# Softmax sums in other banks, and a new order of the steps, in a recurrent memory-attention kernel

## The chip, the cores and the metric

The kernel runs on one core of a Trainium2 chip. The metric is the device time of one execution in microseconds (us). The engines are named as in the profile: PE (TensorE), DVE (VectorE), ACT (ScalarE), POOL (GpSimd) and SP (SyncE, which here issues most DMAs).

## The reference

Two kinds of layer alternate, A B A B, each with a residual sum and a layer norm in front. B (a gated MLP with a product over the sequence) is hardly touched. In A the 2048 rows are cut into 64 segments of 32 rows, and each segment attends over itself and over 8 memory rows, which are the first 8 output rows of the segment before:

```python
for s in range(n_seg):                       # 64 segments, one after the other
    xs = x[:, s * seg_len:(s + 1) * seg_len, :]
    h = jnp.concatenate([mem, xs], axis=1)   # 8 + 32 rows of 512
    q, k, v = (jnp.einsum('btd,dhe->bhte', h, W) for W in (Wq, Wk, Wv))   # 32 heads of 128
    scores = jnp.einsum('bhqe,bhke->bhqk', q, k) * scale
    scores = jnp.where(mask[None, None], scores, -1e9)
    p = _softmax(scores, axis=-1)
    o = jnp.einsum('bhqk,bhke->bhqe', p, v)
    o = jnp.einsum('bhte,hed->btd', o, Wo)
    mem = o[:, :M, :]                        # 8 rows, for the next segment
    outs.append(o[:, M:, :])
```

Weights and activations are bfloat16. So there are 128 segments in a row (64 in each of the two A layers), and each needs the result of the one before.

## The kernel before, in words

`a_block` is one A layer; `segment` (line 830) is one segment. Four segments (j4 = 0 to 3) make a block tb of 128 rows. The program's order on PE, DVE and ACT is the order in which it is written (`manual_schedule`, line 664); POOL's and SP's instructions are placed by the planner.

A segment begins when hA is ready: 32 rows, 8 of memory and 24 of its own, laid out as the stationary side of the projections. (The last 8 rows of each segment are projected ahead, for a whole block, as "old" rows: `b_units`, line 713. Their queries stand in QQ[:, :, :, 32:40], their keys in KX, their values in VX.) Then follow:

- **Projections.** `mm_chunk` (line 674) is 16 matmuls of 512 columns, four 32-column groups of PE by four parts of the contraction. `qk(0)` and `qk(2)` (first half r = 0 of the heads: queries and keys) and `qk(1)` go to three PSUM tiles of a bank each; `k_halves` (line 852) does the keys of the second half in two pieces of 256 columns in banks 0 and 1 of the tile psK; `v_mm(0)` puts the first value chunk into bank 2 of psK. ACT copies queries and keys to SBUF (lines 846, 862), DVE transposes them (lines 850, 864) into QQ and KA.
- **Scores** of both halves (`scores`, line 882, 20 matmuls each, tile psS), then the exponentials on ACT (line 894) into E and the mask on DVE (line 897). E has, per half, 160 columns of (4 heads x 40 rows) and 64 columns for the old rows (`own`). DVE copies the first value chunk (line 968). PE does the second value chunk `v_mm(1)` (psV), which ACT copies (line 980).
- **Softmax sums** by matmuls with ones: `sums_1` (line 899) for half 1 into psM, `sums_0` (line 909) for half 0 into columns 320 to 479 of each bank of psO. Then **PV** (`pv`, line 918) into columns 0 to 319 of psO.
- **Inverses** on ACT, as exp(-ln(sum)): Rm for the 8 memory rows, Rt for the 32 others (`log_of`, line 940, and `inverse`, line 944). DVE multiplies PV by Rm into uT_cur (`scaled`, line 947, source line 948) and later by Rt into uT_nxt (`tok_out`) and oB (`last_out`): the token rows of a segment are projected with the memory rows of the next.
- **Output projection** `wo_pass` (line 743): 128 matmuls into pw, half 1 of the heads first. DVE merges 8 memory rows of pw into the rows of the next segment and transposes them (`build_hA`, lines 821 and 822). ACT copies pw out (`store_o`, line 827), SP stores it.

PSUM's eight banks are used by tags: accA and accB have one bank each, att two, attO four; a tile waits until the readers of its tag's former tile are done. The framework orders accesses of different engines to one PSUM tile.

Between these steps the program puts work that isn't on the recurrence. `fill(n)` does n pieces of the block's projection of old rows (`b_units`, six chunks of 16 matmuls in three segments, in pieces of 4, 4, 8 and 16 matmuls) or of the output projection of old rows (`y_part`). `spare1` (line 1060) is on DVE: a row sum `y_add` (line 223), and at j4 = 3 a normalisation `apply` (line 197). `spare2` is on DVE too: statistics. `copies`, `turns` and `adds` are lists of small jobs of the filling chunks for ACT and DVE. `tail` (line 1092) issues DMAs.

The values of the old rows get into VX through HBM: `spread_v` (line 696) stores VB with one DMA and loads it in 16 DMAs of 16 KB. At the second A layer the old rows of block 0 are projected ahead, at the end of the B layer before (`_Ahead.chunks`, line 609); `wo.open` (line 574) then takes SBUF for Wo and loads it.

## Time and profile before

| | before |
|---|---|
| three runs | 2088.17, 2091.4, 2104.64 us (median 2091.4) |
| the profiled execution | 2106.03 us, span 2104.3 us |
| granted clock of PE, mean | 0.974 |
| busy: PE, PE weight loads, DVE, ACT, POOL | 80%, 50%, 56%, 52%, 8% |
| first and last start of the transpose that writes hA | 30.7 and 1950.5 us (128 of them) |
| DMA queue of SP | 107.17 MB in 205768 packets, 20.2% of 16 engines |

How to read it: the span is the profiled execution from its first to its last instruction. A busy share is a mean over all stages; matmuls are pipelined, so a busy PE need not be a full one. Lines of the timeline have the start in us, the duration, engine, source line, operation, the tiles written and read, the shape, the count, and in brackets the idle time of the engine just before, with what ended it. Lines of a group have busy time and mean duration in ns, and the idle time before them with its releaser. Where a helper makes an instruction, the line is the helper's.

### The profile page before, as it was taken

What the parts mean: (1) busy time and instruction counts of PE and PEld (TensorE: products, weight loads), DVE (VectorE), ACT (ScalarE), POOL (GpSimd) and SP (SyncE); (2) the same over time, 40 slices, a digit from 0 to 9 for tenths busy, and PEclk for the clock granted to TensorE, in tenths of its full rate; (3) what the DMA queues carried; (4) which work ended last, traced back from release to release, by engine and by line L of the source; (5) the groups of instructions that cost most, each with busy time, mean ns of one, the idle gap of its engine ahead of it and who ended that gap; (6) DMA issues with size and microseconds to landing.
All of it is one profiled execution on the core that took longest, in us unless ns stands there. A gap on an engine that the chain in (4) does not pass through costs nothing.

```text
span 2104.3 us, 106502 instructions
## 1 busy us (share of the span) xinstructions
PE 1686.2 (80%) x48827; PEld 1041.7 (50%) x48850; DVE 1170.6 (56%) x2754; ACT 1083.8 (52%) x2530; POOL 164.4 (8%) x388
## 2 busy tenths in 40 slices
PE   3777778887888787889987878887778777887999
PEld 1444445544554444446644544554444444544465
DVE  2455555565555565566455555555565555556742
ACT  1555655554555465554035555555455554555610
POOL 5000000000000000011200000000000000000200
PEclk9899999999999899999999999999999999999999
DMA  9101000011101111137951111011211012021777
GB/s 338 34 19 25 28 25 27 26 45 58 37 27 37 55 52 37 40 112 157 205 154 29 29 29 29 29 29 29 63 59 30 26 48 76 27 49 56 180 157 168
DMA packets 214825, 141.11 MB, mean 67 GB/s; under 512 B 138432, under 2 KB 186928, under 8 KB 214376
## 3 DMA queue, kind: packets, MB, share of 16 engines
q1 hardware_dynamic: 205768, 107.17, 20.2%
q0 software_dynamic: 8592, 27.12, 3.9%
q8 instruction: 382, 6.26, 1.3%
q14 instruction: 67, 0.55, 0.1%
q10 hardware_dynamic: 16, 0.01, 0.0%
HBM read 65.45 MB, written 41.92 MB: 51 GB/s over the span
## 4 chain that ended last, share of the span: by engine, by line
PE 58%; ACT 22%; DVE 13%; DMA 3%; issue 3%; SPq 0%; POOL 0%; DVEq 0%; POOLq 0%
PE pw L746 13%; PE psm L678 9%; PE pg L381 7%; PE psK L678 6%; ACT Rt L942 6%; ACT rows L862 5%; DVE KA L850 4%; PE psK L859 4%; PE pz L280 4%; PE psb L678 3%; ACT Rm L945 3%; ACT Rm L942 3%; ACT rows L846 3%; DVE E L897 2%; DVE uT L948 2%
## 5 line engine op out<-in xcount | busy, mean ns | idle before, releaser
L678 PEld LDWEIGHTS <-hA 128*32 128x32 bf16 x10240 | 266.2, 96 | 337.3 <-issue 104.6
L746 PEld LDWEIGHTS <-uT 128*32 128x32 bf16 x16384 | 259.4, 104 | 272.9 <-DVE uT L948 268.7
L746 PE MATMUL pw<-Wo_high,uT 128*32 128x128 bf16 x8704 | 183.7, 232 | 209.7 <-DVE uT L948 208.6
L846 ACT CAST rows<-psm 128x512 bf16<-128x512 f32 x384 | 225.1, 586 | 166.9 <-PE psm L678 166.8
L678 PE MATMUL psm<-Wq_sb,hA 128*32 128x512 bf16 x4096 | 277.2, 382 | 12.2 <-DVE hA L822 7.6
L948 DVE TENSOR_TENSOR uT<-psO,Rm 128x128 bf16<-128x128 f32 x256 | 62.4, 286 | 336.2 <-ACT Rt L942 336.2
L859 PE MATMUL psK<-Wk_sb,hA 128*32 128x256 bf16 x4096 | 161.4, 273 | 67.3 <-ACT rows L862 67.3
L850 DVE STREAM_TRANSPOSE QQ<-rows 128x512 bf16<-128x512 bf16 x256 | 180.8, 706 | 41.6 <-ACT rows L846 35.2
L678 PE MATMUL psK<-Wv_sb,hA 128*32 128x512 bf16 x2048 | 134.0, 380 | 60.2 <-ACT rows L862 60.2
L894 ACT ACTIVATE E<-psS 128x224 bf16<-128x224 f32 x256 | 77.6, 355 | 202.4 <-PE psS L890 202.4
L859 PEld LDWEIGHTS <-hA 128*32 128x32 bf16 x4096 | 112.4, 96 | 119.3 <-issue 93.3
L945 ACT ACTIVATE Rt<-Rt 128x512 f32<-128x512 f32 x256 | 158.8, 637 | 0.0
L381 PE MATMUL pg<-z,wspT 128*128 128x344 bf16 x1024 | 154.5, 309 | 0.4 <-DMA wspT<-in_B_w_sp_dram 0.4
L827 ACT COPY o_sb<-pw 128x128 f32<-128x128 f32 x126 | 33.5, 266 | 225.7 <-DVE pre L821 222.6
L746 PE MATMUL pw<-Wo,uT 128*32 128x128 bf16 x7680 | 147.3, 234 | 1.4 <-issue 0.7
L862 ACT CAST rows<-psK 128x256 bf16<-128x256 f32 x256 | 96.0, 375 | 92.3 <-PE psK L859 92.2
L948 DVE TENSOR_TENSOR uT<-psO,Rt 128x384 bf16<-128x384 f32 x256 | 139.8, 546 | 2.9
L678 PE MATMUL psm<-Wk_sb,hA 128*32 128x512 bf16 x2048 | 137.6, 381 | 2.5 <-DVE yB L775 2.5
L678 PE MATMUL psV<-Wv_sb,hA 128*32 128x512 bf16 x2048 | 136.1, 382 | 0.0
L968 DVE CAST VA<-psK 128x512 bf16<-128x512 f32 x128 | 88.5, 691 | 85.4 <-PE psK L678 85.4
L821 DVE CAST_PREDICATED pre<-maskM,pw 128x128 bf16<-128x128 uint16 x126 | 36.6, 291 | 174.5 <-PE pw L746 174.5
L864 DVE STREAM_TRANSPOSE KA<-rows 128x256 bf16<-128x256 bf16 x256 | 108.5, 424 | 41.5 <-ACT rows L862 41.3
(170 smaller groups left out, 2594.0 us busy)
## 6 DMA issues: line engine op xcount, KB each, us to landing
vb_d<-front SPq DMA_DIRECT2D x32, 256.0 KB
VX<-vb_d SPq DMA_DIRECT2D x512, 16.0 KB
o_d<-o_sb SPq DMA_DIRECT2D x126, 64.0 KB
ln_x<-xd SPq DMA_DIRECT2D x26, 256.0 KB
y_o<-o_d SPq DMA_DIRECT2D x22, 256.0 KB
xd<-y_o SPq DMA_DIRECT2D x22, 256.0 KB
y_x<-xd SPq DMA_DIRECT2D x22, 256.0 KB
Wq_sb<-in_A_Wq_dram POOLq DMA_DIRECT2D x8, 512.0 KB, 8.4
```

The source lines that it names most:

```text
L381: nc.tensor.matmul(pg[t][:, k, 0:344], lhsT=wsp[t][:, st, :], rhs=z(st, 344 * k, 344 * k + 344), start=(st == 0), stop=(st == NT - 1))
L678: nc.tensor.matmul(ps[32 * cg:32 * cg + 32, :], lhsT=lhs(kt, cg), rhs=rhs(kt, cg), start=(kt == 0), stop=(kt == KT - 1), tile_position=(0, ...
L746: nc.tensor.matmul(po[32 * cg:32 * cg + 32, 0:128], lhsT=lhs[:, _place(h), :], rhs=wo_rhs(h, cg), start=(h == WO_ORDER[0]), stop=(h == WO_ ...
L846: nc.scalar.copy(r[:], ps)
L850: nc.vector.transpose(out=QQ[:, j % 2, :, 0:32] if j < 2 else KA[:, j % 2], in_=r[:])
L859: nc.tensor.matmul(o[32 * cg:32 * cg + 32].rearrange("p (i c) -> p i c", i=2), lhsT=hA_cur[:, kt, :], rhs=qk_rhs(w, 3, kt, cg)[:, 2 * a:2 ...
L862: nc.scalar.copy(r[:, 256 * a:256 * a + 256], o)
L864: nc.vector.transpose(out=KA[:, 1, 8 * a:8 * a + 8], in_=r[:, 256 * a:256 * a + 256])
L942: nc.scalar.activation(out=t, in_=sview(r, lo, hi), func=ACT.Ln)
L945: nc.scalar.activation(out=t[:, r], in_=t[:, r], func=ACT.Exp, scale=-1.0)
L948: nc.vector.tensor_tensor(out=out, in0=o, in1=t[:, r].rearrange("p (g i q) -> p g i q", g=4, i=4)[:, :, :, lo:hi], op=ALU.mult)
L968: nc.vector.tensor_copy(VA[:, 0].rearrange("p i e -> p (i e)"), psK[:, 2, :])
```

## The change

- **Sums.** `sums_memory` (8 matmuls of 64 columns) sums only for the 8 memory rows, both halves, into columns 320 to 383 of psO's banks, ahead of PV. `sums_tokens` (8 matmuls) sums for the 32 other rows, both halves, into the two banks of a tile of its own, psT. ACT's logarithms become one for Rm (from psO, ahead of PV) and one for Rt (1024 columns, from psT).
- **Orders dropped.** `other_bank` tells the framework that a set of matmuls need not wait for a given read of the same tile, since it is in another bank: `qk(2)` against the copy of `qk(0)`, `v_mm(0)` against the copy of `qk(3)`, `scores(1)` against `exps(0)`.
- **Order of the segment.** The four query and key chunks run one after the other, and the keys of the second half are one chunk again. `scores(0)` and `exps(0)` come before `v_mm(0)`; then two pieces of filling, `scores(1)`, `exps(1)`, `v_mm(1)`, and `spare1`. The copy of the first value chunk goes from DVE to ACT, that of the second from ACT to DVE. Half 0 of the heads goes first in the scaling, the projection and the token rows; `last_out` is one operation for both halves.
- **Filling.** The chunks of `b_units` all use accA (the first block of the first layer apart); the value chunks come first and both in the first of the three segments.
- **Values of the old rows.** VX belongs to the Wo pools now. For block 0 of either layer it is filled on DVE by transposes (`regroup`), not through HBM. For later blocks the store comes a segment earlier and the 16 loads are issued 8 and 8 in the `tail` of segments j4 = 2 and 3.

```diff
-WO_ORDER = tuple(range(H // 2, H)) + tuple(range(H // 2))
...
+    def regroup(self, VB, VX):
+        for r in range(2):
+            t = self.rows.pool.tile([P, DM], BF16, name="ln_xn", bufs=2)
+            self.nc.vector.transpose(out=t[:], in_=VB[:, :, r, :])
+            t = t[:].rearrange("p (i b j k) -> p j b i k", i=4, b=4, j=4)
+            for j in range(4):
+                self.nc.vector.transpose(out=VX[:, j, r, :], in_=t[:, j])
...
-        for pair in ((0, 2), (1, 3), (4, 5)):
+        for pair in ((4, 5), (0, 2), (1, 3)):
...
+        def other_bank(mms, *reads):
+            for m in mms:
+                for r in reads:
+                    tc.declare_no_dep(m.ins, r.ins, reason="another bank of the tile")
...
-            for k, j in enumerate((0, 2, 1, 3, 4, 5) if early else (4, 0, 5, 2, 1, 3)):
-                if (early and k < 4) or k % 2 == 0:
-                    ps = (accA if k % 2 == 0 else accB).tile([P, 512], F32, name="psb")[:]
-                else:
-                    ps = att.tile([P, 512], F32, name="psb2")[:]
+            for k, j in enumerate((0, 2, 1, 3, 4, 5) if early else (4, 5, 0, 2, 1, 3)):
+                ps = (accB if early and k in (1, 3) else accA).tile([P, 512], F32, name="psb")[:]
...
+            def sums_memory(ps):
+                for k in range(2):
+                    for g in range(4):
+                        nc.tensor.matmul(ps[:, g, 320:384], lhsT=ones[32 * g:32 * g + 32, :],
+                                         rhs=e_own(32 * g, 32, 0) if k else e_all(32 * g, 32, 0, 8),
+                                         start=(k == 0), stop=True, tile_position=(32 * g, 0), skip_group_check=True)
+            def sums_tokens(ps):
+                for k in range(2):
+                    for sl in range(2):
+                        for g in range(2):
+                            o = ps[:, g, 256 * sl:256 * sl + 256].rearrange("p (n q) -> p n q", q=32)
+                            nc.tensor.matmul(o[:, :, 24:32] if k else o, lhsT=onesG[64 * g:64 * g + 64, sl, :],
+                                             rhs=e_own(64 * g, 64, 1) if k else e_all(64 * g, 64, 8, 40),
+                                             start=(k == 0 and sl == 0), stop=True, skip_group_check=True)
...
-            r0 = qk(0, accB.tile([P, 512], F32, name="psm")[:])
-            r2 = qk(2, accA.tile([P, 512], F32, name="psm")[:])
+            psQ = att.tile([P, 2, 512], F32, name="psQ")
+            r0, _, read = qk(0, psQ[:, 0, :])
+            r2, mms, _ = qk(2, psQ[:, 1, :])
+            other_bank(mms, read)
             qk_T(0, r0)
             qk_T(2, r2)
-            r1 = qk(1, att.tile([P, 512], F32, name="psm1")[:])
+            r1, _, _ = qk(1, accB.tile([P, 512], F32, name="psm")[:])
+            qk_T(1, r1)
             psK = attO.tile([P, 4, 512], F32, name="psK")
-            k1 = k_halves(psK)
-            ...
-            v_mm(0, psK[:, 2, :])
-            nc.vector.tensor_copy(VA[:, 0].rearrange("p i e -> p (i e)"), psK[:, 2, :])
+            r3, _, read = qk(3, psK[:, 0, :])
             psS = att.tile([P, 2, 512], F32, name="psS")
-            for r in range(2):
-                scores(r)
-            ...
+            scores(0)
+            expd = exps(0)
+            qk_T(3, r3)
+            close(0)
+            other_bank(v_mm(0, psK[:, 1, :]), read)
+            nc.scalar.copy(VA[:, 0].rearrange("p i e -> p (i e)"), psK[:, 1, :])
+            fill(2)
+            other_bank(scores(1), expd)
+            exps(1)
+            close(1)
             psW = accB.tile([P, 512], F32, name="psV")
             v_mm(1, psW)
-            fill(2 if first and s == 0 else 1)
-            nc.scalar.copy(VA[:, 1].rearrange("p i e -> p (i e)"), psW[:])
+            nc.vector.tensor_copy(VA[:, 1].rearrange("p i e -> p (i e)"), psW[:])
+            spare1()
...
             psO = attO.tile([P, 4, 512], F32, name="psO")
-            sums_0(psO)
+            sums_memory(psO)
+            Rm = segp.tile([P, 4, 64], F32, name="Rm", bufs=1)
+            nc.scalar.activation(out=Rm[:], in_=psO[:, :, 320:384], func=ACT.Ln)
+            nc.scalar.activation(out=Rm[:], in_=Rm[:], func=ACT.Exp, scale=-1.0)
+            psT = att.tile([P, 2, 512], F32, name="psT")
+            sums_tokens(psT)
             for r in range(2):
                 pv(r, psO)
-            ...
+            fill()
+            Rt = segp.tile([P, 4, 256], F32, name="Rt", bufs=1)
+            nc.scalar.activation(out=Rt[:].rearrange("p g n -> p (g n)"), in_=psT[:].rearrange("p g n -> p (g n)"), func=ACT.Ln)
...
             def tail():
+                if j4 in (2, 3) and tb + 1 < NB:
+                    for j in (0, 1):
+                        spread_v(blk_state[tb + 1], 2 * j4 - 4 + j)
```

## The prediction

> **What bounds the kernel now.** I read the page first: who is busy, and by whom the chain is made.

> ```profile
> span 2104.3 us, 106502 instructions
> PE 1686.2 (80%) x48827; PEld 1041.7 (50%) x48850; DVE 1170.6 (56%) x2754; ACT 1083.8 (52%) x2530; POOL 164.4 (8%) x388
> PE 58%; ACT 22%; DVE 13%; DMA 3%; issue 3%; SPq 0%; POOL 0%; DVEq 0%; POOLq 0%
> ```

> No engine is full, and the chain goes to and fro between PE, ACT and DVE: a recurrence of short dependent steps. The steps are the 128 segments. The ends of the transposes that write hA (line 822) lie 888.7 us apart from first to last in the first layer and 882.5 us in the second: 1771.2 us for 126 steps, 84% of the span. Cleanest steps take 13.0 us. Second view: the timeline of one segment; its first query matmul starts at 457.43.

> ```profile
> 460.03 0.61 PE L859 MATMUL psK<-Wk_sb,hA 128*32 128x256 bf16 x16
> 460.74 0.38 ACT L862 CAST rows<-psK 128x256 bf16<-128x256 f32 x1
> 461.17 0.62 PE L859 MATMUL psK<-Wk_sb,hA 128*32 128x256 bf16 x16 [0.53 <-ACT rows L862]
> ...
> 462.26 1.05 PE L678 MATMUL psK<-Wv_sb,hA 128*32 128x512 bf16 x16 [0.47 <-ACT rows L862]
> ...
> 463.71 0.61 ACT L894 ACTIVATE E<-psS 128x224 bf16<-128x224 f32 x2 [1.50 <-PE psS L890]
> ...
> 464.54 0.59 ACT L980 CAST VA<-psV 128x512 bf16<-128x512 f32 x1 [0.22 <-PE psV L678]
> ...
> 464.69 0.37 PE L906 MATMUL psM<-E,onesG 64*128 64x160 bf16 x8
> 464.99 0.28 PE L915 MATMUL psO<-E,ones 32*128 32x160 bf16 x8
> ...
> 466.26 0.58 ACT L942 ACTIVATE Rt<-psM 128x512 f32<-128x512 f32 x1
> 466.73 0.59 ACT L942 ACTIVATE Rt<-psO 128x512 f32<-128x512 f32 x1
> ...
> 467.36 0.49 DVE L948 TENSOR_TENSOR uT<-psO,Rm 128x128 bf16<-128x128 f32 x2 [2.13 <-ACT Rt L942]
> 467.70 1.08 PE L746 MATMUL pw<-Wo_high,uT 128*32 128x128 bf16 x64 [1.36 <-DVE uT L948]
> ```

> PE stands three times. The second half of the keys, and then the first value chunk, write psK only after ACT's copy out of another bank of psK: 0.53 and 0.47 us. After the sums PE has 0.36 us of PV and a piece of filling work and then stands until 467.70: DVE's scaling of the memory columns needs only PV and the inverse of the memory sums, ready at 466.35, but it reads psO, and ACT is still reading token sums of slice 0 out of psO until 467.32. From the first sum to the output projection it is 3.01 us. The groups say that this holds for all segments:

> ```profile
> L948 DVE TENSOR_TENSOR uT<-psO,Rm 128x128 bf16<-128x128 f32 x256 | 62.4, 286 | 336.2 <-ACT Rt L942 336.2
> L859 PE MATMUL psK<-Wk_sb,hA 128*32 128x256 bf16 x4096 | 161.4, 273 | 67.3 <-ACT rows L862 67.3
> ```

> **The rows I use.** A chunk of 16 matmuls holds PE for 0.865 us (starts 458.31 and 459.17). From PE's last start of a chunk's pace to ACT or DVE it is 0.23 us more; ACT to DVE 0.03; either to PE 0.05. A copy of 512 columns is 0.586 on ACT, 0.691 on DVE; a transpose of 512 0.706; an exponential of E 0.355; a mask 0.319; the scaling of 128 memory columns 0.286; Wo's 128 matmuls 1.80 (529.73 to 531.53 in the segment that starts at 519.47). On ACT and DVE an independent follower starts 0.09 us before the end. With these the old order, laid out instruction by instruction, gives a step of 13.07 us, beside the 13.0 seen; so I trust the same bookkeeping for the new one.

> **Front half of the segment, new.** Time 0 is the first query matmul. The four chunks run without a stop and end at 3.46: the halves of the keys are gone, and the order against ACT's read of the other bank is dropped. ACT copies the last at 3.69 to 4.28, DVE transposes it 4.31 to 5.01. Meanwhile PE does the scores of slice 0 (0.16: 20 matmuls, half of 463.12 to 463.45), the first value chunk to 4.49 and two pieces of filling (0.43) to 4.92, so the wait for the keys' transpose is covered but for 0.14. Where there is no filling (first segment of early blocks) that cover is gone, and PE waits 0.57 at the same place, with no later end. Scores 1 end at 5.22, exponential 5.45 to 5.81, mask 5.84 to 6.16, sums from 6.21; the second value chunk lies behind the scores and ends at 6.09. Before, the sums began at 464.69, so at 7.26: **1.05 us gained**. The copy of the first value chunk moves to ACT, between the two exponentials: 4.72 to 5.30, done before the second has its scores (5.45). The other copy goes to DVE, 6.32 to 7.01.

> **Back half, new.** Memory sums: 8 matmuls of 64 columns, 0.11 as the 8 of slice 0 now take (464.99 to 465.10). Added wait: PV, and behind it filling and projection, now waits for ACT's logarithm over the same banks. It starts at 6.55; 256 columns lie between 0.278 (128) and 0.579 (512), on the line 0.378: done at 6.92. The token sums fill that time: between 0.30 as now and 0.43 (1280 columns for 896); I take 0.43, to 6.75. PV 6.97 to 7.37, with the second half's values ready at 7.01 while its matmuls start at 7.17. Memory inverse done at 7.37 (0.419, between 0.310 and 0.637). Scaling 7.60, projection 7.94: 1.73 after the first sum instead of 3.01, **1.28 us gained**. The token logarithm (one of 1024 columns, 0.98 as the two of 512 take) is off that path, since it reads its own banks. Projection to hA is unchanged: it ends at 9.74, the filling chunk at 10.60, hA at 10.60. **A step is 10.65 us**, 2.42 less than 13.07. PE's own work in it is 9.98, so it is nearly the bound.

> [...] The 8 of slice 0 start 14 ns apart here. [...]

> **Added or moved work that may show.** (a) All filling now goes through accA, one bank: the last chunk waits for ACT's copy of the piece before, done at 9.43 against 9.74. A margin of 0.3, cost nothing; if ACT is later, PE is late by the excess. (b) DVE: row sums and normalisation (0.68 and 0.41) now stand between the value copy and the scaling, and two statistics (0.86 each) ahead of the merge into hA; laid out, blocks with both lose 0.7 per four steps, some 17 of 32 blocks: +12. (c) SP: the 16 VX loads of a block, 0.6 to 0.69 each, go 8 and 8 to the ends of two segments. Now they hold up a row load in four steps:

> ```profile
> 478.02 3.37 SPq L702 DMA_DIRECT2D VX<-vb_d  x5
> ...
> 482.59 0.64 SPq L219 DMA_DIRECT2D y_o<-o_d  x1
> 485.77 0.69 DVE L223 TENSOR_TENSOR y_o<-y_o,y_x 128x512 f32<-128x512 f32 x1 [7.77 <-DMA y_o<-o_d]
> ```

> These four steps are 32.4 us over. With 8 loads (5.2 us) instead of 16 ahead, the row arrives some 10 us into the segment, 3 to 4 late: 17 left, bounds 0 and 50. (d) Regrouping the first values on DVE: 2 x (0.706 + 4 x 0.311) = 3.9, once per layer. In the first layer it replaces 8.4 us of waiting for VX (49.3 to 57.8) and saves perhaps 6; at the second it falls among DVE work that PE doesn't wait for, bounds 0 and 3.9, taken as 2. POOL's queue is passed by nothing. (e) Instruction fetch. The chain shows such stops:

> ```profile
> 505.34 1.00 issue
> ```

> Above 13.07 per step the 126 steps hold 124 us: 32.1 in the two first ones, 32.4 for the rows, 59.7 else, mostly such stops. PE's idle time falls from 3.2 to 0.7 us a step, so stops hidden now will show. Bounds: -10 (a few instructions fewer) and +126 (a stop of 1.0 in each step); nearest to what is seen, 0.47 a step, I add +30.

> **The sum.** 126 x 10.65 = 1342; firsts 26; rows 17; stops 90; DVE 12; regrouping 2: 1489 for 1771, so -282. The profiled execution took 2106.0, so 1824; it lies 0.7% above the median of the three runs (2091.4). Scaled alike: **1812 us**. Its own range is 1765 to 1860.

> **Rivals.** *Fetch takes it*: PE, without pauses, stops 1.0 us in each step. For: pauses are where fetches hide. Against: most fetches pass without a stop even through the projection. +96 on the sum: 1907 us. *The dropped orders remain* in effect, that is, the change doesn't do what it says, and PE waits for each read of a neighbouring bank: the layout gives 12.08 a step, +180: 1990. Against: the waits above are exactly between such reads and writes of one tile. *Slower*, by one mechanism: denser matmuls bring the granted clock down. The place is PE's 9.98 us a step; at 0.75 they are 13.31, a step 13.98, about 2227. It decides from a step of 12.89, that is from a clock of 0.82. Against: a stretch with PE 81% busy (520 to 533) is granted 1.00, and the low clock, 0.63, is at 478 to 492, around the 7.8 us wait; idleness, not density, brings it.

> [...]

> **Numbers.** Forecast 0.64, fetch 0.17, orders 0.13, no change 0.02, slower 0.04. The first three are faster by over 1% (about what a measurement here can tell from no change): 0.94. The range, 1765 to 1895, takes the forecast's own and reaches half way into the fetch case.

> **What would show it.** Right: steps of 10.6 to 11.1 us; no wait of the memory scaling for a token logarithm; no wait of PE between the key chunks and the first value chunk; PE over 85% busy; sums to projection about 1.7 us. Wrong: a step over 11.5; PE waiting for ACT's copy ahead of the last filling chunk; DVE's row sum waiting for its load in more than four steps; "issue" above 6% of the chain; a lower clock.

## The result, and the profile after

The kernel after takes 1821.6 us (1819.2 to 1823.8), the kernel before 2095.3 us (2088.2 to 2104.6): a ratio of 0.869 with a 95% interval of 0.865 to 0.873, so 274 us less. The profiled execution after took 1823.8 us. From the page of the kernel after, the lines on the span, on who is busy, on the queue that brings instructions (packets, MB, share), and on the chain:

```profile
span 1822.1 us, 101610 instructions
PE 1652.9 (91%) x46779; PEld 959.6 (53%) x46802; DVE 1136.2 (62%) x2518; ACT 1037.1 (57%) x2018; POOL 164.0 (9%) x388
q8 instruction: 366, 6.00, 1.4%
PE 80%; issue 6%; DVE 5%; DMA 4%; ACT 4%; POOL 0%; SPq 0%; DVEq 0%; ACTq 0%; POOLq 0%
```

PE's busy time hardly falls; its idle time does. ACT goes from 22% of the chain to 4%, DVE from 13% to 5%: PE is the bound now. What doubles, from 3% to 6%, is "issue", time in which an engine waits for nothing that the profile shows. The timeline of one of the cleanest steps; its first query matmul starts at 551.75 (columns: start, duration, engine, line, operation, and in brackets the idle time before it and what ended that):

```profile
551.75 1.05 PE L689 MATMUL psQ<-Wq_sb,hA 128*32 128x512 bf16 x16
...
554.35 1.04 PE L689 MATMUL psK<-Wk_sb,hA 128*32 128x512 bf16 x16
...
555.34 1.03 PE L689 MATMUL psK<-Wv_sb,hA 128*32 128x512 bf16 x16
...
556.05 0.71 DVE L864 STREAM_TRANSPOSE KA<-rows 128x512 bf16<-128x512 bf16 x1 [0.15 <-ACT rows L861]
...
556.82 0.28 PE L887 MATMUL psS<-QQ,KA 128*32 128x40 bf16 x16
...
557.93 0.24 PE L912 MATMUL psO<-E,ones 32*128 32x64 bf16 x8
...
558.10 0.45 PE L922 MATMUL psT<-E,onesG 64*128 64x256 bf16 x8
558.22 0.38 ACT L985 ACTIVATE Rm<-psO 128x256 f32<-128x256 f32 x1 [0.66 <-PE psO L912]
...
558.64 0.42 ACT L986 ACTIVATE Rm<-Rm 128x256 f32<-128x256 f32 x1
558.66 0.28 PE L930 MATMUL psO<-E,VA 32*128 32x40 bf16 x16
...
558.96 1.00 ACT L993 ACTIVATE Rt<-psT 128x1024 f32<-128x1024 f32 x1
...
559.35 0.49 DVE L995 TENSOR_TENSOR uT<-psO,Rm 128x128 bf16<-128x128 f32 x2 [0.61 <-PE psO L934]
559.70 1.02 PE L761 MATMUL pw<-Wo,uT 128*32 128x128 bf16 x60
```

First sum 6.18 us after the first query matmul (7.26 before), projection 1.77 after the first sum (3.01 before). The first value chunk (555.34) has no wait ahead of it. DVE scales (559.35) while ACT is still in the logarithm of the token sums (558.96 to 559.96), which before had to end first. The groups say it for all segments (busy, mean ns of one, idle time before and what ended it):

```profile
L995 DVE TENSOR_TENSOR uT<-psO,Rm 128x128 bf16<-128x128 f32 x256 | 62.5, 285 | 65.4 <-PE psO L934 65.2
L689 PE MATMUL psK<-Wv_sb,hA 128*32 128x512 bf16 x2048 | 135.4, 380 | 0.0
L222 DVE TENSOR_TENSOR y_o<-y_o,y_x 128x512 f32<-128x512 f32 x24 | 16.4, 684 | 7.5 <-DMA y_o<-o_d 7.5
```

The scaling waited 336.2 us for ACT before; now it waits 65.2 us, and for PE. From the first to the last hA of each layer the 126 steps take 741.2 + 745.7 = 1486.9 us (before 1771.2): 284 us less, while the rest of the span is 2 us longer. So the gain is all in the steps. Their cleanest are 10.66 us, but their median is 11.58 in the first layer and 11.81 in the second.

### The profile page after: what moved, and what is told of

Its sections match the earlier page's. It is cut to its first block, busy times and chain, and to the rows that moved or that the text cites. A ratio compares the mean times of both kernels' runs of the same rounds, so it can differ in the third digit from the quotient of the medians.

```text
span 1822.1 us, 101610 instructions
## 1 busy us (share of the span) xinstructions
PE 1652.9 (91%) x46779; PEld 959.6 (53%) x46802; DVE 1136.2 (62%) x2518; ACT 1037.1 (57%) x2018; POOL 164.0 (9%) x388
## 4 chain that ended last, share of the span: by engine, by line
PE 80%; issue 6%; DVE 5%; DMA 4%; ACT 4%; POOL 0%; SPq 0%; DVEq 0%; ACTq 0%; POOLq 0%
PE pw L761 15%; PE psQ L689 12%; PE psK L689 11%; PE psb L689 8%; PE pg L380 8%; PE psm L689 6%; PE psV L689 4%; PE pz L279 4%; PE pwB L773 3%; ACT Rm L985 3%; PE psO L930 3%; PE psS L887 3%; PE py L423 2%; PE psO L912 1%; DMA wspT<-in_B_w_sp_dram 1%
## 5 line engine op out<-in xcount | busy, mean ns | idle before, releaser
L861 ACT CAST rows<-psQ 128x512 bf16<-128x512 f32 x256 | 149.8, 585 | 130.4 <-PE psQ L689 130.4
L864 DVE STREAM_TRANSPOSE KA<-rows 128x512 bf16<-128x512 bf16 x256 | 181.4, 709 | 37.1 <-ACT rows L861 32.3
L689 PE MATMUL psQ<-Wq_sb,hA 128*32 128x512 bf16 x2048 | 139.7, 382 | 13.4 <-DVE hA L837 7.8
L689 PE MATMUL psQ<-Wk_sb,hA 128*32 128x512 bf16 x2048 | 140.3, 381 | 2.1 <-issue 1.9
L689 PE MATMUL psm<-Wq_sb,hA 128*32 128x512 bf16 x2048 | 138.9, 380 | 0.5 <-issue 0.5
L689 PE MATMUL psK<-Wk_sb,hA 128*32 128x512 bf16 x2048 | 138.1, 379 | 0.0
L380 PEld LDWEIGHTS <-wspT 128*128 128x128 bf16 x1024 | 100.7, 98 | 59.0 <-DMA wspT<-in_B_w_sp_dram 5.0
L899 DVE TENSOR_TENSOR E<-E,maskN 128x224 bf16<-128x224 bf16 x256 | 72.2, 282 | 95.0 <-ACT E L896 95.0
L993 ACT ACTIVATE Rt<-psT 128x1024 f32<-128x1024 f32 x128 | 128.7, 1005 | 0.0
L689 PEld LDWEIGHTS <-hB 128*32 128x32 bf16 x2976 | 75.4, 97 | 83.5 <-DVE hB L613 25.2
```

The lines of the kernel that those rows point to most:

```text
L380: nc.tensor.matmul(pg[t][:, k, 0:344], lhsT=wsp[t][:, st, :], rhs=z(st, 344 * k, 344 * k + 344), start=(st == 0), stop=(st == NT - 1))
L689: return [nc.tensor.matmul(ps[32 * cg:32 * cg + 32, :], lhsT=lhs(kt, cg), rhs=rhs(kt, cg), start=(kt == 0), stop=(kt == KT - 1), tile_posi ...
L861: return r, mms, nc.scalar.copy(r[:], ps)
L864: nc.vector.transpose(out=QQ[:, j % 2, :, 0:32] if j < 2 else KA[:, j % 2], in_=r[:])
L899: nc.vector.tensor_tensor(out=E[:, r], in0=E[:, r], in1=maskN[:], op=ALU.mult)
L993: nc.scalar.activation(out=Rt[:].rearrange("p g n -> p (g n)"), in_=psT[:].rearrange("p g n -> p (g n)"), func=ACT.Ln)
```

## The experiments

All ratios are to the kernel before. "Step" is the mean of the 122 steps behind the first two of each layer. "Stops" needs a word. A pause is counted here from one start on PE to the next, so it is somewhat longer than the idle time in the brackets of a timeline. In the kernel after, of 80 pauses of PE over 0.45 us that nothing in the profile ends, 79 fall at one place of PE's instruction stream, within each layer the same modulo 256 (matmuls, weight loads and the sequencer's instructions counted); in the kernel before all 23 do. The column is the sum, over the 126 steps, of unexplained pauses over 0.3 us at that place.

That PE waits there for its instructions can be read from the packets of the queue q8. The kernel after has 46779 matmuls, 46802 weight loads and 109 sequencer instructions on PE, 93690 in all, which fill 366 times 256 places, and q8 has 366 packets of 16 KB. Matched in order, one packet to a place, nowhere in its steps does PE pass such a place sooner than 1.1 us after the end of its packet, and every long stop at one ends 1.1 to 1.7 us after it.

| kernel | us | ratio (95%) | step, us | us per 256 PE instructions | stops, us |
|---|---|---|---|---|---|
| before | 2095.3 | 1 | 13.82 | 4.82 | 26 |
| new back half only | 2015.4 | 0.960 (0.956-0.964) | 13.10 | 4.57 | 98 |
| new front half only | 2037.3 | 0.968 (0.963-0.973) | 13.20 | 4.81 | 11 |
| after, orders kept | 1981.1 | 0.944 (0.940-0.948) | 12.85 | 4.69 | 89 |
| after | 1821.6 | 0.869 (0.865-0.873) | 11.61 | 4.23 | 98 |
| after, wide projection | 1721.0 | 0.820 (0.817-0.822) | 10.87 | 5.46 | under 3 |
| back half, wide projection | 1909.7 | 0.909 (0.906-0.912) | 12.29 | 5.81 | under 3 |
| before, wide projection | 2067.9 | 0.984 (0.982-0.986) | 13.50 | 6.38 | 3 |
| first padding, "good" place | 1900.3 | 0.904 (0.901-0.907) | 12.32 | 4.11 | 157 |
| first padding, "bad" place | 1911.6 | 0.910 (0.907-0.913) | 12.31 | 4.10 | 170 |
| second padding, "good" place | 1850.8 | 0.881 (0.878-0.883) | 11.88 | 3.96 | 111 |
| second padding, "bad" place | 1900.7 | 0.905 (0.902-0.908) | 12.20 | 4.07 | 156 |
| front half, pause filled | 1923.9 | 0.917 (0.914-0.919) | 12.46 | 4.25 | 30 |
| after, VX loads together | 1821.8 | 0.868 (0.866-0.869) | 11.59 | 4.23 | 96 |

The theory at the start was the prediction's sum: both halves of the segment get shorter, and instruction fetch takes some of it back. The rivals: the dropped orders do all of it; the halves are worth little by themselves; the fetch stops are something else.

### Parts of the change

**New back half only**: the old kernel with the memory sums, the token sums and their inverses as in the new one, and half 0 of the heads first (the edit is shortened here).

```diff
-            sums_1(psM); sums_0(psO)          # and the four logarithms of slices 1 and 0
+            sums_memory(psO)                  # one logarithm of 256 columns, one inverse
+            sums_tokens(psT)                  # own banks; one logarithm of 1024 columns
...
```

> The old kernel with the new back half alone: memory sums ahead of PV in psO's spare columns, token sums in psT, one logarithm each, half 0 first in scaling and projection. The front half of the segment, its fillings and the VX loads are the old ones. My theory (two cuts on one path that add): first sum to projection falls from 3.0 to 1.75 us, the clean step from 13.0 to about 11.75 us, the time to about 1955 us (1935 to 1975). Rival (the back half is all of the gain, the front's new order only shifts waits): about 1830 us. Rival (the steps gain from the front, the sums were hidden anyway): about 2090 us.

2015.4 us. The cleanest steps are 11.79, as laid out, but the run is 60 us over what was expected. The waits of PE (total, times, longest):

```profile
PE psK L859 <- ACT rows L862: 67.2, 128, 0.8
PE psK L678 <- ACT rows L862: 60.1, 128, 0.5
PE pw L746 <- issue: 56.0, 57, 2.0
```

The first two lines are the front's waits, which this kernel keeps. The third is new: the projection stops in 57 places with no releaser, 56 us. Stops went from 26 to 98 us, as many as in the full change. The mechanism of the back half is right, and some 70 us of its gain are eaten by fetch.

**New front half only**: the new kernel with the old sums, inverses and order of heads (the edit is shortened).

```diff
-            sums_memory(psO)
-            sums_tokens(psT)
+            sums_1(psM)
+            sums_0(psO)
...
```

> The new kernel with the old back half: sums of half 1 in psM, of half 0 in psO, memory logarithm of half 0 behind PV, half 1 first. Front half, dropped orders, fillings and VX loads are the new ones. My theory: the clean step goes from 10.67 to about 11.95 us, since DVE again waits for ACT's token logarithm in psO; the time to about 1950 us (1930 to 1985). Rival (the back half is all of the gain): about 2090 us. Rival (the front is all): about 1825 us. Theory and both rivals together: the two halves' gains, measured against the old kernel, sum to the whole, 274 us, if they lie on one path one after the other.

2037.3 us, nearly 90 over the expectation. Part of it is a wait that the layout had not seen:

```profile
PE pw L762 <- DVE uT L951: 204.8, 128, 2.2
...
PE psO L925 <- DVE VA L984: 12.9, 81, 0.2
```

The first is the old pause ahead of the projection, kept. The second is PV, which comes earlier behind the sums here than DVE's copy of the second values: 0.16 us in 81 steps, so cleanest steps of 12.11 to 12.19 for 11.95. The rest is the clock. The granted clock is 0.935 on the mean; with stretches of 1 and of 0.5 alone, as the trace has them, that is 2 x 0.065 x 2019 = 262 us at half speed (before 0.974, 109 us; after 0.993, 26 us), and half of the steps have 13.66 to 13.88 us. Six stretches of this kernel (columns: stretch, its length, PE busy and matmuls, granted clock, DMA share, GB/s):

```profile
503.20:506.61 3.41, 1.68 (x92) 1.00 0.11 29
506.61:510.02 3.41, 3.41 (x120) 0.50 0.10 29
510.02:513.43 3.41, 3.41 (x68) 1.00 0.27 96
513.43:516.85 3.42, 3.40 (x104) 1.00 0.36 105
516.85:520.26 3.41, 1.67 (x88) 1.00 0.27 77
520.26:523.67 3.41, 3.41 (x128) 0.50 0.05 12
```

In this trace the clock changes in stretches of 3.41 us. Each of the two in which PE is busy for half of it (1.68 and 1.67 us) is followed by one at half speed (0.50), where the projection then is slow: in a step further on it takes 3.44 us (602.45 to 605.89), in the old kernel at full clock 1.98 (529.73 to 531.71). That makes the step 13.65 us long, which is four stretches, so the pause meets the same place of the next stretch again: the kernel is locked to it.

**Front half, pause filled**: this theory of the clock, tested with work that fills the pause and gives nothing (its bank is started anew by the projection).

```diff
+            for k in range(24):
+                g = k % 4
+                nc.tensor.matmul(pw[32 * g:32 * g + 32, :], lhsT=c["zeros"][:], rhs=wo.high[:, 0, :],
+                                 start=(k < 4), stop=(k > 19), tile_position=(0, 32 * g))
             wo_pass(pw, uT_cur)
```

> The new front half with the old back half, and 24 matmuls of 512 columns by zero weights in the pause ahead of the projection (their bank is started anew by the projection). Theory (the pause of 1.5 us comes at the same place of each 3.41 us window of the clock, since the step is four windows long, and the half clock that follows holds the step at that length): no window at half clock, steps 12.1 to 12.2 throughout, time 1955 to 1980 for 2037. Rival (the clock has nothing to do with the pause): 2037 or, with the added matmuls late, more.

1923.9 us: 113 us less, by adding 24 matmuls of 512 columns to every step, and below the expected range. The clock is 0.998, the median step 12.25. The same stretches:

```profile
503.20:506.61 3.41, 3.41 (x164) 1.00 0.02 5
506.61:510.02 3.41, 3.41 (x88) 1.00 0.09 24
510.02:513.43 3.41, 3.24 (x116) 1.00 0.02 5
```

So with the pause filled the front half is 171 us faster than the old kernel, without it 58, and what hid the difference was the clock. How much of the 171 the filling would give the old kernel, which has 109 us at half speed of its own, no run shows.

**After, with the orders between banks kept**: nothing of the schedule is changed, only the declarations dropped.

```diff
         def other_bank(mms, *reads):
-            for m in mms:
-                for r in reads:
-                    tc.declare_no_dep(m.ins, r.ins, reason="another bank of the tile")
+            pass
```

> The new kernel with all three dropped orders kept (the declaration is left out), all else new. My theory: the second query or key chunk waits for ACT's copy of the first, the first value chunk for the copy of the last key chunk, the second scores for the first exponential; laid out this gives a clean step of 12.08 instead of 10.67 us, and 1821 + 126 x 1.41, less some 30 us of fetch stops that hide in the new pauses: about 1970 us (1950 to 2000). Rival (the order of the steps does it, and the waits between banks were short enough to hide): below 1850 us.

1981.1 us, cleanest steps 12.08, both as the layout had it. PE waits for ACT's read of the neighbouring bank, at the second chunk and at the first value chunk:

```profile
PE psQ L689 <- ACT rows L859: 88.2, 128, 0.9
PE psK L689 <- ACT rows L859: 70.4, 127, 0.6
```

The third dropped order, at the second scores, shows no wait for ACT. With the orders kept 159.5 of the 273.7 us are lost; the rest of the change alone gives 114.2.

### The stops

**After, with a wide projection**: 32 matmuls of 512 columns in place of 128 of 128, the same columns in all. PE's step has about 511 instructions in place of 703 (the expectation says 539 and 731). This kernel and the next two leave out the sum over the four partial results.

```diff
-            for h in range(H):
-                for cg in range(4):
-                    nc.tensor.matmul(po[32 * cg:32 * cg + 32, 0:128], lhsT=lhs[:, _place(h), :], rhs=wo_rhs(h, cg), ...)
+            for i in range(H // 4):
+                for k in range(4):
+                    nc.tensor.matmul(po[32 * k:32 * k + 32, :], lhsT=lhs[:, _place(4 * i + k), :], rhs=..., ...)  # 512 columns
```

> The new kernel with the output projection as 32 matmuls of 512 columns instead of 128 of 128: each quadrant of pw gets the product of every fourth head over all columns, and the sum over the four quadrants is left out, so the projected rows are partial sums. PE's columns stay the same (32 x 54 ns = 1.73 us for 1.80), its instructions fall from about 731 to 539 a step. My theory: the stops of PE without a releaser (106 us in the 126 steps, 62 of them at the projection) are waits for instructions; most of those at the projection go: about 1750 us (1735 to 1770). Rival (the stops come from something that goes with the work, not with the count of instructions): 1821 - 9, about 1812 us.

1721.0 us, still below what was expected. From its page:

```profile
span 1721.0 us, 77034 instructions
q8 instruction: 270, 4.42, 1.1%
PE 83%; DVE 6%; DMA 5%; ACT 4%; issue 2%; POOL 0%; SPq 0%; DVEq 0%; ACTq 0%; POOLq 0%
```

No pause of PE over 0.45 us is left without a releaser. The cleanest steps hardly change (10.61 for 10.66), so it is not that the projection got shorter; the median does (10.7 for 11.6 to 11.8). 96 fetches fewer, and the stops are gone.

**The wide projection in the old kernel, and with the new back half** (the same edit).

> The old kernel with the projection in 32 matmuls of 512 columns (the sum over its four partial results is left out). Theory: the old kernel has only some 26 us of fetch stops, since its pause ahead of the projection hides them, so it gains little: 2045 to 2075, and the change is worth some 335 us where no fetch stops it, against 276 where it does. Rival (the wide projection gains some 100 us in any kernel): 1990 to 2005.

> The old front half with the new back half, and the projection in 32 matmuls of 512 columns in place of 128 of 128 (the sum over its four partial results is left out). Theory (the new back half alone gained 82 us and not more because its steps run into fetch stops): stops fall from 115 us to below 25, clean step 11.7, time 1895 to 1920. Rival (the wide projection gives what it gives by shortening the projection, 0.04 us a step): 2005 to 2015.

2067.9 and 1909.7 us, both as expected. In kernels without stops the change is worth 2067.9 - 1721.0 = 347 us: 158 for the back half and 189 for the front on top of it. (The clock has a part in these: the three kernels have 99, 66 and 30 us at half speed.) With stops it is worth 274. The 73 us between them are the growth of the stops, 98 - 26 = 72. That is where this part of the gain went.

**Padding, first try.** If place decides, steps of 768 instructions, three times 256, would keep the boundaries at chosen places. Matmuls by zero weights fill up each step.

```diff
             sums_tokens(psT)
+            pads(psT)      # 20 to 50 matmuls of 40 columns by zeros, start=False
```

> The new kernel with 20 to 50 matmuls of 40 columns by zero weights (they add nothing to the token sums) put behind the token sums in each step, so many that each step has 768 instructions on PE, three times 256, and the places of the stops lie at the same three points of each step: 93 instructions into the projection, and 256 and 512 instructions before that. Theory (PE stops for its instructions at every 256th, and is late for it only where it has just run through instructions quickly, behind the first 100 or so of the projection): more work, but hardly a stop. Clean step about 10.75 us, stops below 20 us in all for 106, time 1715 to 1755. Rival (the wide projection gained by having fewer instructions and weight loads, not by where the fetches fall): 1830 to 1840, stops as before or more.

> The same padding with 128 matmul and weight-load instructions shifted, so that one of the three places of each step lies 221 instructions into the projection, close to its end. Theory: one stop of some 1.2 to 1.4 us in each step at the same place: 126 times 1.2 above the well-placed version, 1860 to 1930. Rival (number of instructions, not place): the same as the well-placed version within 15 us.

1900.3 and 1911.6 us. The "good" place was a miss, and above its rival too. The "bad" one lies in its range, but by luck: it is within 11 us of the good one, which is the rival's case. The good one stops in each step at the boundary inside the projection:

```profile
469.56 0.40 PE L498 MATMUL pw<-Wo,uT 128*32 128x128 bf16 x14 [0.86 <-issue]
...
481.80 0.40 PE L498 MATMUL pw<-Wo,uT 128*32 128x128 bf16 x13 [1.09 <-issue]
...
494.04 0.40 PE L498 MATMUL pw<-Wo,uT 128*32 128x128 bf16 x14 [1.09 <-issue]
```

The pads are quick instructions (64 in 0.4 us) and stand right ahead of other quick ones. In the steps, no kernel has more than 1 in 100 spacings from one fetch packet to the next under 3.33 us. So a second theory: 256 instructions take at least some 3.5 us, and a stretch that needs less stops for what is lacking.

**Padding, second try**: the pads where PE waits for the keys' transpose anyway, and between long instructions.

```diff
+            other_bank(pads(psS), expd)      # into the bank that the second scores start anew
             other_bank(scores(1), expd)
```

> The new kernel with about 32 matmuls of 40 columns by zero weights again, now ahead of the second scores, where PE waits 0.4 us for the keys' transpose and where the instructions around are long ones (they write zeros where the scores then start anew). The step has 768 instructions on PE again, and the boundaries of 256 lie 96 instructions into the projection, and 256 and 512 before that. Theory, made after the first padding failed (256 instructions of PE take no less than about 3.5 us, since the fetch of the next 256 lasts so long; a stop is what is lacking): by the start times of the cleanest step of the new kernel the three stretches of 256 last 3.7, 3.5 and 3.3 us, so a stop of 0 to 0.3 us a step, step 10.7 to 10.9, time 1725 to 1770. Rival (added instructions cost a stop wherever they stand): about 1900, as the first padding.

> The same with the boundaries 151 instructions later, at 247 instructions into the projection. Theory (256 instructions take no less than 3.5 us): the projection and its nearest neighbours fill one stretch of 256, which would last 1.8 to 2.2 us, and another falls short too; together 2.0 to 2.5 us of stops in each step: 1980 to 2050. Rival: as the well-placed version.

1850.8 and 1900.7 us: the theory is wrong in both directions. The good place has a stop in most steps, many at the second scores or the value chunk behind them, in a stretch that by itself was laid out as long enough, and the bad place has fewer than laid out (156 us where 2.0 to 2.5 a step would be 252 to 315). From the good one and from the bad one:

```profile
476.07 0.19 PE L498 MATMUL psS<-QQ,KX 128*32 128x64 bf16 x1 [0.50 <-issue]
```

```profile
472.08 0.27 PE L498 MATMUL pw<-Wo_high,uT 128*32 128x128 bf16 x5 [0.67 <-issue]
...
484.39 0.24 PE L498 MATMUL pw<-Wo_high,uT 128*32 128x128 bf16 x4 [1.08 <-issue]
```

In the good one the profile puts 43.6 us of PE's waits at the second value chunk down to ACT's exponential. Most of these stand at the place modulo 256, and ACT had ended 0.15 to 0.9 us before PE went on; those are counted as stops.

What the four paddings have in common is in the table: 3.96 to 4.11 us per 256 instructions, that is, steps of three fetches that last 11.9 to 12.3, wherever the boundaries lie and whether the pads cost PE anything or not. The kernel after, with 2.75 fetches a step, has 4.23; the wide one has 5.46 and doesn't stop. Below about 4 us per 256 no kernel here has come. The place decides the rest, 11 us in the first pair and 50 in the second.

In the other kernels this mean doesn't order the stops: 89 us at 4.69 us per 256 with the orders kept, but 11 at 4.81 in the new front half alone, and 30 at 4.25 with its pause filled. What they differ in is the pause ahead of the projection. PE's waits without a releaser at the projection, before, after, and with the orders kept:

```profile
PE pw L746 <- issue: 1.8, 3, 1.1
```

```profile
PE pw L761 <- issue: 51.3, 52, 1.5
```

```profile
PE pw L759 <- issue: 48.7, 53, 1.6
```

The new back half alone has 56.0 us of them, the front half alone none, and 4.8 with its pause filled. So the three kernels that keep the 1.6 us ahead of the projection, idle or filled with long matmuls, hardly stop in the projection, whose 256 instructions PE runs in 1.8 us; the three that have lost it do. The pauses between the chunks, which the kernel with the orders kept has back (88.2 and 70.4 us in all), don't hide the stops (89 us). Why the paddings come to about 4.0 where single fetches follow each other at 3.4 is open, and no version that does all of the work without the stops was found.

### The loads of VX

**After, with the 16 VX loads together behind the store**, as before the change.

```diff
                         elif j == 5:
                             store_v(bs)
+                            for jj in range(4):
+                                spread_v(bs, jj)
...
-                if j4 in (2, 3) and tb + 1 < NB:
-                    for j in (0, 1):
-                        spread_v(blk_state[tb + 1], 2 * j4 - 4 + j)
```

> The new kernel with all 16 loads of VX behind the store, as before the change, in place of 8 and 8 at the ends of two steps. Theory (the row sum waits behind these loads in SP's queue): waits of 6 to 8 us for y_o in the steps where a row load comes behind them, four to eight times, 1845 to 1880. Rival (the shorter wait comes from the other changes of the order): 1815 to 1828.

1821.8 us, and the row sum waits 8.6 us in all: the rival. The prediction's reason for the shorter wait is wrong. SP's queue around the same block, before (its step starts at 457.38), after (389.46) and in this kernel (392.14):

```profile
468.34 0.32 SPq L698 DMA_DIRECT2D vb_d<-front  x1
470.40 10.99 SPq L702 DMA_DIRECT2D VX<-vb_d  x16
...
482.59 0.64 SPq L219 DMA_DIRECT2D y_o<-o_d  x1
```

```profile
390.30 0.33 SPq L713 DMA_DIRECT2D vb_d<-front  x1
392.71 9.57 SPq L719 DMA_DIRECT2D VX<-vb_d  x14
...
405.88 1.46 SPq L218 DMA_DIRECT2D y_o<-o_d  x1
```

```profile
392.98 0.33 SPq L713 DMA_DIRECT2D vb_d<-front  x1
395.75 10.94 SPq L719 DMA_DIRECT2D VX<-vb_d  x16
...
409.03 0.32 SPq L218 DMA_DIRECT2D y_o<-o_d  x1
```

The store of the values went from 11.0 us into the step to 0.8, and in the kernel after, too, 14 of the 16 loads follow it in one row, though the program issues them 8 and 8. The new order of the filling chunks (4, 5, 0, 2, 1, 3 for 4, 0, 5, 2, 1, 3) makes the second values the second chunk and not the third, some 10 us earlier, so that the loads are through before the row is wanted. The new back half by itself, which has the old order of chunks, keeps the four long steps: 20.2 to 21.7 us. No run changes the order of chunks alone.

## Why the prediction was right, and where it was not

The forecast was 1812 us, the time 1821.6; of the cases it was the forecast's own. Its sum was made for the profiled execution, and there it says 1824 for 1823.8. By its steps:

| part | predicted | measured |
|---|---|---|
| first query matmul to first sum | 6.21 | 6.18 |
| first sum to projection | 1.73 | 1.77 |
| clean step | 10.65 | 10.66 |
| two first steps, above clean | 26 | 24.6 |
| rows, in 126 steps (measured: DVE's wait) | 17 | 7.5 |
| everything else, in 126 steps | 104 (stops 90, DVE 12, regrouping 2) | 112 |
| 126 steps | 1489 | 1486.9 |

- **The clean step** held in every part, and with it the kernels of parts: 11.79 without the front, 12.08 with the orders kept. Without the back it is 12.11 to 12.19, for 11.95.
- **The scaling to the median** failed. The profiled execution before was 0.5% above the final median, the one after only 0.1%, so 12 us were taken off where 2 were right. That is the miss of 9.6 us. (1824 so scaled is 1811; the prediction has 1812.)
- **The stops** came out near by luck: two errors cancel. What was 59.7 us in the old kernel was called "mostly such stops"; at boundaries of 256 there are 26. The rest of it was not taken apart, but that kernel has 109 us at half clock. And the growth was put at 30 us, between -10 and +126; it is 72. Stops went to 98 while the half clock went to 26 us, and the sum stayed. The 14 us beside the stops weren't taken apart, so the 12 for DVE and the 2 for regrouping are not shown. With so much of PE's idle time gone, the 0.47 us a step seen in the old kernel, where pauses hide fetches, was the wrong row to lean on.
- **Where a fetch hides** was right in its main point, that pauses hide it, but it didn't say which: the one ahead of the projection does (26, 11 and 30 us of stops in the three kernels that have it, idle or filled; 98, 98 and 89 in the back half alone, after, and with the orders kept). The rival "fetch takes it", 1.0 us a step, was the right mechanism, at 0.78 us a step in all (98 over 126).
- **The rows** were right in sign, wrong in reason: the order of chunks, not the halving of the loads.
- **Memory sums.** They took 0.17 us up to the first token sum (557.93 to 558.10); the forecast took 0.11. The 8 matmuls use four groups of 32 rows in turn; within each four they start 3 to 4 ns apart, the second four start 29 ns behind the first, and 0.12 us pass from the last to the first token sum. The forecast's 14 ns is a mean of the same kind: 3 to 4 ns within a four, 69 between. It cost 0.06 us a step, and the clean step didn't show it.
- **Orders remain** (1990) is refuted by the waits, and was a good price: the kernel that keeps them took 1981.
- **Slower by the clock** is refuted, as the prediction had argued: PE is busier, 91% for 80%, and the granted clock rose from 0.974 to 0.993; in the front half alone the half clock follows stretches with PE half idle (1.68 of 3.41 us busy). The rival's 0.75 was an assumption that no run shows.
- **What would show it.** PE is busy 91%, no wait of the scaling for a token logarithm, none ahead of the value chunk. But the test "steps of 10.6 to 11.1" is met by clean steps only; the mean by the forecast's own sum was 11.8, so it was badly put. By the same token its sign of being wrong, "a step over 11.5", is met by the measured mean of 11.8. "Issue", at 6%, is at the limit that was set for it.

## What to carry to other kernels

Price a change of order from the clean step, laid out instruction by instruction, and then ask what the removed pauses did: here the one ahead of the projection hid instruction fetches (26 us of stops with it, 98 without), and in the front half alone a pause of 1.6 us a step was long enough to halve the clock of the stretch behind it (1.00 to 0.50). Where an engine nears its bound, count its instructions, not only their time: 703 in a step of 10.7 us were not all fetched in time (98 us of stops in 126 steps), and a projection in a quarter of the instructions ran the median step (10.7 us) close to its laid-out length (10.65). Two halves of a change measured alone add up only if neither falls into another limit: 80 and 58 us alone were 274 together.
